# The same instructions in another order: ScalarE and VectorE take turns on the PSUM tile of q and the exponentials

## The chip, the core and the metric

The kernel runs on one core of a Trainium2 chip, in one launch. The metric is the device time of that launch in microseconds; less is better. A core has five engines, each with an instruction line of its own that it works through strictly in order: TensorE (PE in the profile, its weight loads are PEld), VectorE (DVE), ScalarE (ACT), GpSimd (POOL), and SyncE (SP), which here issues all transfers between the chip's memory (HBM) and SBUF. An instruction that needs the result of another engine waits at the head of its engine's line, and everything behind it waits too.

## The reference

One transformer block for 2048 tokens of width 512, in fp32: layer norm, sliding dilated attention (32 heads of 16, eight keys at distance 0, 2, ..., 14), residual, layer norm, a GEGLU feed-forward of width 1792, residual.

```python
qkv = layernorm(x) @ wqkv                      # split into q, k, v, 32 heads of 16
idx = pos[:, None] - 2 * arange(8)[None, :]    # eight keys for each position
logits = einsum("bhsd,bhswd->bhsw", q, k[idx]) * 16 ** -0.5    # masked where idx < 0
o = einsum("bhsw,bhswd->bhsd", softmax(logits), v[idx])
h = x + o @ wo
out = h + (gelu(layernorm(h) @ w_gate) * (layernorm(h) @ w_up)) @ w_down
```

## The kernel before

The tokens are split into four blocks of 512 (numbered 0 to 3). Even and odd positions are kept apart, so that the dilated window is eight rows next to each other. A block passes through projection of q, k and v (L675 to L825), attention (L829), output projection with residual and second layer norm (tail, L931), and the feed-forward. Blocks 0 and 1 run the feed-forward in 14 steps each (ffn_step, L1014), beside the attention of the block after next to them; blocks 2 and 3 run it together with fewer products (early_step L1403, joint L1131, last_sums L1320). Matrix products are made of three matmuls each, of a high and a low part of both operands; the casts to the high part are ScalarE's (L409), the subtraction that gives the low part is VectorE's or GpSimd's (L410).

TensorE has no part in the attention itself. For each of four groups of eight heads, ScalarE copies two rows of q into the tile qp in PSUM (L854), VectorE multiplies them with eight keys (L861, names pk) and adds up over the head's 16 places (L864, into lg). VectorE or GpSimd mask lg (L875), VectorE takes the largest (L877), VectorE or GpSimd subtract it (L878); ScalarE reads one element of it to bring in the exponential's table early (a dummy activation, L881) and writes the exponentials into qp (L883); VectorE sums them (L884), inverts the sum (L886), scales (L887), multiplies with eight values (L903, names pv), and adds these up in three steps by itself or on GpSimd (L908, L910). Tile qp has two halves of 256 values to a partition, taken by groups of heads in turn; both lie in one PSUM tile.

```python
qp = T("qp", [P, 2, 2 * QF], name="qp", pool=psum)
...
i = b % 2
...
act(310, lambda q=q, jj=jj: nc.scalar.copy(
    qp()[:, i].rearrange("p (j f) -> p j f", j=2), q()[:, jj:jj + 2, :]), qrs, [(qp, i)])
```

In a feed-forward step TensorE makes pg and pu from the weights gu (L498), ScalarE takes the gelu of pg into g (L1047), VectorE multiplies g with pu (L1053), ScalarE and GpSimd or VectorE split g into gh and gl (L409, L410), and TensorE adds the product with the down weights to acc (L996 to L998), two steps later. The two banks for pg and pu are taken in turn, so the next step's matmuls need the last step's L1047 and L1053. Weights come from HBM as fraw; ScalarE casts them (L409, L1011, L1025). The low parts of the weights are computed once, written to HBM and read back (ld).

The order is written out. Every operation is recorded by Plan.add (L265) in the program's order with its number; PLACES (L62) holds one number for each of the 2853 operations, and Plan.schedule (L303) sorts the operations by it and emits them in that order, which sets each engine's line. SWAPS lists operations that run on the other of their two possible engines (Plan.swap, L297). Semaphores are set by the layer below, from which instruction touches which tile, in the order of emission.

Of the kernel before, what the change touches and what calls it, by code (L numbers as in the profile page):

```python
# [62 lines left out]
    4765, 17791, 0, 825, 1032, 1239, 1446, 1653, 1860, 2067, 2274, 2481, 2688, 2895, 3102, 3309, 3516, 3723, 3930, 4137, 4344, 4551, 4758, 4965, 5172,  # L63
    5379, 5586, 5793, 6530, 7479, 7589, 7699, 8263, 11601, 28478, 14543, 11401, 26924, 29078, 38112, 40916, 470, 1410, 7001, 8296, 1880, 7857, 8901, 0,
    940, 6146, 6911, 2350, 8712, 10151, 3290, 2820, 3760, 11278, 11938, 4700, 13196, 15673, 5170, 13844, 16923, 4230, 15440, 18748, 20748, 5291, 5291,
    5921, 6611, 6171, 7031, 7526, 10732, 7255, 8382, 11688, 7251, 8206, 4435, 4435, 5000, 5621, 5721, 6041, 6911, 10392, 6306, 7866, 8901, 12118, 12852,
    11072, 12028, 12496, 14292, 14950, 17528, 9568, 10302, 10512, 11348, 12006, 15588, 13188, 13543, 15443, 8036, 8744, 8971, 9652, 10106, 10333, 10560,
    12022, 12930, 13384, 14066, 14968, 15966, 7809, 8517, 9198, 9425, 9879, 10787, 11014, 11796, 12250, 12476, 17238, 19280, 19816, 15648, 15876, 16102,
    16330, 16556, 16784, 17010, 17464, 19734, 19960, 20414, 21548, 21986, 12704, 13158, 13612, 13838, 14740, 15194, 15422, 17692, 18826, 19052, 19506,
    20188, 20624, 22710, 28513, 26633, 27573, 7990, 28618, 29808, 7520, 19291, 19951, 7050, 17266, 28064, 8460, 25014, 25674, 17918, 20642, 24496, 27438,  # L70
    21776, 23590, 25404, 28028, 27218, 28124, 32202, 34270, 22682, 26310, 29482, 32587, 5640, 18133, 19968, 6580, 19353, 25416, 8930, 22341, 25326, 6110,
    20178, 25236, 27124, 27478, 29032, 29692, 13188, 21201, 14448, 22956, 25538, 26924, 22576, 24096, 26488, 28668, 33320, 34404, 31296, 35830, 38552,
    39918, 30388, 33110, 34016, 40508, 36738, 40366, 41272, 42390, 34924, 37644, 39458, 42980, 43704, 45584, 45114, 44174, 9400, 32914, 37358, 40934,
    19808, 31664, 36202, 36862, 40134, 40594, 43174, 45480, 41820, 48894, 46294, 46954, 19338, 38312, 43570, 44230, 23180, 30414, 38762, 41540, 42484,
    43514, 48204, 50144, 44330, 50834, 51638, 52298, 18868, 23526, 24292, 20278, 30182, 30948, 27103, 31956, 35480, 23650, 36726, 37882, 39562, 39916,
    43552, 45486, 42180, 46820, 44908, 58034, 49466, 51048, 52652, 54024, 55606, 60394, 56768, 58350, 64536, 66170, 48094, 50152, 59512, 61094, 55396,
    56978, 62256, 58140, 59722, 63960, 60884, 62466, 65908, 67490, 63662, 64602, 64132, 63192, 74982, 68740, 68270, 69210, 46280, 47188, 50838, 68933,
    44002, 51746, 63628, 68033, 72744, 73652, 74558, 75884, 70024, 70930, 71838, 75294, 77078, 78018, 76608, 77548, 48330, 53548, 60312, 61644, 50270,
    55488, 63756, 64960, 66170, 67550, 68364, 70304, 69523, 70994, 76474, 78806, 53674, 65564, 74768, 75676, 52210, 62894, 72048, 72954, 74330, 76620,
    77300, 78116, 77080, 84356, 78930, 80056, 28043, 39286, 41098, 31804, 44854, 49430, 36336, 52164, 52930, 44644, 53786, 58940, 59798, 64144, 68652,  # L80
    79456, 67280, 87685, 81838, 83858, 75466, 85488, 87070, 91190, 88232, 89814, 94628, 96358, 78652, 80746, 90976, 92558, 83210, 84792, 89604, 86860,
    88915, 91850, 92348, 93930, 96000, 97582, 96066, 94656, 95126, 95596, 99302, 98362, 101102, 98832, 76838, 80930, 93720, 99497, 77744, 80024, 84582,
    100207, 101488, 102394, 103302, 105614, 104208, 105116, 106022, 107140, 108804, 108334, 109274, 107864, 63056, 81336, 82415, 92507, 94520, 95754,
    64282, 72572, 73652, 82590, 90714, 91970, 93910, 95414, 98810, 100906, 96210, 96870, 101366, 108586, 80046, 85382, 90850, 101892, 103512, 111182,
    86326, 87970, 89050, 104036, 106324, 107336, 110162, 110842, 111906, 112366, 111906, 113056, 113636, 114452, 98744, 107730, 97372, 118546, 111464,
    113046, 100116, 114208, 115790, 119206, 116952, 118534, 124309, 131641, 112836, 114418, 119745, 121327, 115580, 117648, 122713, 118373, 119955,
    124541, 121341, 125333, 129309, 130891, 126998, 127938, 126058, 127468, 132891, 132421, 139225, 139695, 106930, 107836, 110558, 134840, 108744,
    109650, 133402, 137290, 141106, 142013, 142920, 151884, 138844, 139751, 144275, 146025, 233320, 159029, 189713, 188773, 26163, 46054, 29144, 30414,
    32738, 35170, 35614, 37940, 34522, 50740, 34860, 43514, 45840, 47410, 48034, 50580, 42144, 42604, 46170, 65390, 47720, 50240, 52774, 53164, 53624,
    56738, 60394, 66860, 55830, 59254, 69054, 76960, 77606, 78958, 91240, 97679, 99500, 52680, 58154, 60838, 61754, 68490, 68623, 70684, 73010, 54798,  # L90
    58694, 64620, 95046, 65080, 68150, 75204, 76280, 79506, 81996, 85606, 87546, 77300, 88236, 90720, 93220, 96734, 99772, 108320, 112431, 116196, 65072,
    83745, 82280, 82725, 85490, 87660, 88360, 93218, 81306, 84930, 86856, 100087, 90404, 90850, 97018, 98242, 98702, 101246, 105436, 106646, 101806,
    104296, 106042, 110502, 110962, 112041, 116380, 119124, 121282, 98120, 101246, 103606, 106204, 105304, 106646, 107106, 107496, 107956, 115056, 116802,
    118546, 112246, 117406, 119866, 120592, 121117, 121551, 121996, 124085, 125023, 125468, 109744, 122923, 123583, 90380, 123448, 126083, 117862, 123973,
    124833, 117392, 124498, 126688, 121327, 126588, 127495, 128402, 129519, 130244, 131551, 131761, 132116, 133310, 133895, 134975, 138279, 143386,
    144046, 125681, 130681, 131588, 132705, 133775, 134510, 134720, 135075, 135760, 136345, 137425, 140794, 142551, 143291, 132495, 134309, 135216,
    136830, 137555, 138290, 138500, 138855, 139681, 136123, 137030, 137937, 139054, 140146, 140881, 141091, 141446, 142196, 140658, 142061, 142686,
    143827, 144485, 145110, 122656, 78488, 150450, 131499, 145715, 148040, 148040, 150235, 153045, 116922, 96536, 118332, 120545, 122336, 127293, 143076,
    155240, 158610, 156494, 158050, 158730, 178238, 160215, 162883, 163343, 163733, 164193, 166738, 173548, 174923, 166738, 169098, 170358, 172858,
    175738, 176818, 191227, 194519, 204608, 148730, 156309, 169063, 170123, 171183, 173658, 179758, 181328, 184138, 161410, 162323, 166398, 192999,  # L100
    166858, 170238, 173388, 175853, 176313, 180613, 187243, 191573, 178518, 190433, 197953, 201233, 205193, 206273, 210523, 212840, 215053, 143521,
    170003, 180843, 182498, 187848, 192133, 190392, 194328, 197138, 189743, 191573, 193513, 206138, 195044, 199938, 201233, 202668, 206548, 212023,
    213768, 214713, 203128, 205858, 209468, 214373, 215173, 216253, 219775, 223076, 225823, 199938, 201503, 202668, 208498, 203483, 205333, 206278,
    208753, 209213, 215658, 217403, 218128, 218008, 221318, 227373, 228583, 218943, 219600, 222392, 223601, 227033, 229043, 229700, 234030, 236573,
    237018, 154180, 158695, 153690, 139779, 126528, 130974, 138380, 140269, 140971, 131809, 136225, 143991, 140165, 145182, 146089, 146996, 147903,
    148810, 149717, 148350, 152440, 153165, 155244, 138755, 144975, 145635, 146615, 148135, 145500, 146885, 149510, 148260, 150624, 151531, 152438,
    153345, 154252, 155159, 154670, 157445, 158170, 160805, 141696, 150834, 151494, 151359, 152744, 150255, 153994, 155839, 164415, 156066, 156973,
# [1436 lines left out]
```

## Time and profile before

| what | before |
|---|---|
| median of three runs | 626.97 us (624.17 to 627.29) |
| the profiled execution's own time | 625.67 us |
| its span, first to last instruction | 623.9 us |
| weight loads of TensorE | 499.9 us busy |
| mean rate of the transfers | 248 GB/s, 154.51 MB |
| granted TensorE clock | 1.00 |

The span is what the trace covers; the 1.8 us beside it lie around the first and the last instruction. Busy time of an engine counts its instructions' own time. A matmul's end is modelled and overlaps the next one's start, so that the distance from start to start tells TensorE's pace. In the views of the prediction a row names the engine, the line of the kernel, the tile written and, behind an arrow, the tiles read, without buffer numbers; the idle time of an engine before an instruction stands with the instruction or transfer that ended it.

### The profile page before, as it was taken

The page shows a single profiled execution, that of the slowest core. Times are in us where ns is not written, and L with a number is a line of the kernel's source. Part 1 is how long each engine was busy: PE and PEld are TensorE (multiplying, and loading weights), DVE is VectorE, ACT ScalarE, POOL GpSimd, SP SyncE. Part 2 cuts the span into 40 slices and gives each one's busy share as a digit, 9 for nine tenths or more (in the row PEclk, how much of TensorE's full clock was granted, in tenths as well). Part 3 has the DMA queues.
Part 4 walks back from the last instruction along what each step waited for, and adds up shares of the span by engine and source line. Part 5 has one row for each costly group of instructions (what it writes and reads, how often), then busy time and mean ns, then how long its engine had stood idle before and what let it go on. Part 6 is the DMA issues. An engine that isn't in the chain of part 4 may idle for free.

```text
span 623.9 us, 8388 instructions
## 1 busy us (share of the span) xinstructions
PE 610.5 (98%) x2696; PEld 499.9 (80%) x2696; DVE 534.4 (86%) x674; ACT 440.5 (71%) x765; POOL 349.4 (56%) x327
## 2 busy tenths in 40 slices
PE   8999999999999899999999999999999999999997
PEld 7888788887877778887888878888777888888885
DVE  6889999989989898999999899747978887778862
ACT  5787598748456766796886869789865675568841
POOL 5589897525888845766484683304124433443562
PEclk9999999999999999999999999999999999999999
DMA  8758588689998898979999889967489655758984
GB/s 297 229 178 299 191 241 231 179 274 301 342 267 297 255 291 278 285 234 336 334 318 342 245 235 275 311 181 217 129 235 260 225 195 176 221 163 238 245 237 119
DMA packets 106365, 154.51 MB, mean 248 GB/s; under 512 B 47296, under 2 KB 60352, under 8 KB 105936
## 3 DMA queue, kind: packets, MB, share of 16 engines
q1 hardware_dynamic: 106320, 153.97, 79.6%
q8 instruction: 21, 0.34, 0.2%
q14 instruction: 24, 0.20, 0.1%
HBM read 107.48 MB, written 36.23 MB: 230 GB/s over the span
## 4 chain that ended last, share of the span: by engine, by line
PE 65%; DMA 12%; DVE 6%; ACT 6%; POOL 5%; issue 4%; SPq 1%; DVEq 0%; ACTq 0%; POOLq 0%
PE dn L1316 10%; PE pa L1198 8%; DMA fraw<-in_wffn_dram 8%; PE qkv L498 7%; PE pu L498 6%; PE pg L498 5%; PE wo L498 5%; PE pc L1198 5%; PE qka L757 4%; PE acc L996 2%; PE acc L997 2%; PE acc L998 2%; PE qkc L757 2%; PE qkv L491 2%; DMA gu<-ld 1%
## 5 line engine op out<-in xcount | busy, mean ns | idle before, releaser
L861 DVE TENSOR_TENSOR pk<-kw,qp 128x2048 f32<-128x2048 f32 x32 | 72.9, 2280 | 4.5 <-ACT qp L854 3.1
L903 DVE TENSOR_TENSOR pv<-vw,qp 128x2048 f32<-128x2048 f32 x32 | 72.6, 2281 | 3.0 <-ACT qp L883 1.4
L864 DVE TENSOR_REDUCE lg<-pk 128x128 f32<-128x2048 f32 x32 | 72.7, 2274 | 0.2
L908 POOL TENSOR_TENSOR pv<-pv 128x512 f32<-128x512 f32 (+1 forms) x36 | 65.6, 1831 | 11.0 <-DVE pv L903 7.4
L498 PE MATMUL pu<-hTh,gu 128*128 128x512 f32 x224 | 60.3, 391 | 2.8 <-DVE g L1053 2.8
L498 PE MATMUL pg<-hTh,gu 128*128 128x512 f32 x224 | 60.2, 390 | 0.8 <-DMA gu<-ld 0.5
L498 PEld LDWEIGHTS pu<-hTh,gu 128*128 128x128 f32 x224 | 41.8, 188 | 12.7 <-DVE g L1053 4.1
L498 PEld LDWEIGHTS pg<-hTh,gu 128*128 128x128 f32 x224 | 41.8, 188 | 10.4 <-DMA gu<-ld 0.9
L996 PE MATMUL acc<-dnh,gh 128*128 128x512 f32 x112 | 43.6, 389 | 0.0
L997 PE MATMUL acc<-dnl,gh 128*128 128x512 f32 x112 | 43.6, 389 | 0.0
L998 PE MATMUL acc<-dnh,gl 128*128 128x512 f32 x112 | 43.6, 389 | 0.0
L410 POOL TENSOR_TENSOR gu<-fraw,gu 128x512 fp32r<-128x512 f32 x21 | 27.1, 1298 | 20.4 <-ACT gu L409 14.3
L410 POOL TENSOR_TENSOR gl<-g,gh 128x512 fp32r<-128x512 f32 x23 | 30.0, 1304 | 14.5 <-ACT gh L409 14.4
L910 POOL TENSOR_TENSOR o<-pv 128x256 f32<-128x256 f32 x25 | 21.3, 856 | 26.7 <-DVE pv L908 14.8
L1198 PE MATMUL pa<-tt,jh 128*128 128x512 f32 x112 | 30.3, 393 | 0.9 <-ACT gr_xhat L1223 0.7
L498 PE MATMUL pu<-hTl,gu 128*128 128x512 f32 x112 | 30.0, 389 | 0.0
L498 PE MATMUL pg<-hTl,gu 128*128 128x512 f32 x112 | 29.9, 389 | 0.0
L908 DVE TENSOR_TENSOR pv<-pv 128x1024 f32<-128x1024 f32 (+1 forms) x28 | 29.6, 1072 | 0.1
L1228 ACT COPY jt<-pa 128x512 f32<-128x512 f32 x32 | 18.7, 585 | 12.3 <-PE pa L1198 10.3
L409 ACT CAST gu<-fraw 128x512 fp32r<-128x512 f32 x28 | 16.8, 617 | 14.0 <-DMA fraw<-in_wffn_dram 13.0
L477 POOL TENSOR_SCALAR rs_h<-mv_h 128x1 f32<-128x1 f32 x16 | 4.6, 291 | 39.0 <-DVE mv_h L476 38.9
L1198 PEld LDWEIGHTS pa<-tt,jh 128*128 128x128 f32 x112 | 20.8, 188 | 6.3 <-ACT gr_xhat L1223 1.1
(496 smaller groups left out, 1834.0 us busy)
## 6 DMA issues: line engine op xcount, KB each, us to landing
fraw<-in_wffn_dram SPq DMA_DIRECT2D x47, 768.0 KB, 6.0
kw<-kv SPq DMA_DIRECT2D x16, 704.0 KB, 6.0
vw<-kv SPq DMA_DIRECT2D x16, 704.0 KB, 6.4
gu<-ld SPq DMA_DIRECT2D x19, 512.0 KB, 5.6
kv<-qkvt SPq DMA_DIRECT2D x32, 256.0 KB, 3.1
ld<-gu SPq DMA_DIRECT2D x14, 512.0 KB, 5.2
ws<-sums_kw SPq DMA_DIRECT2D x21, 256.0 KB, 2.2
x<-in_x_dram SPq DMA_DIRECT2D x16, 256.0 KB, 5.4
```

The lines of the kernel that those rows point to most:

```text
L410: sub = lambda eng: eng.tensor_tensor(lo(), src(), hi().bitcast(F32), op=ALU.subtract)
L498: nc.tensor.matmul(acc(), a, b, start=(p == k == 0 and not seeded), stop=(p == n - 1 and k == KD - 1), skip_group_check=seeded)
L757: nc.tensor.matmul(acc(), a(k), b()[:, k], start=first and q == k == 0, stop=q == 2 and k == 1, skip_group_check=not first)
L861: nc.vector.tensor_tensor(pr(), k4, q2.unsqueeze(2).to_broadcast([P, 2, W, QF]), op=ALU.mult)
L864: dve(2195, lambda pr=pr, jj=jj: nc.vector.tensor_reduce(lg()[:, i, jj:jj + 2], pr().rearrange("p j w (h d) -> p j w h d", d=DH), axis=AX. ...
L903: nc.vector.tensor_tensor(pr().rearrange("p j w (h d) -> p j w h d", d=DH), v5, e5, op=ALU.mult)
L908: either(home, 256 * m, lambda eng, pr=pr, m=m: eng.tensor_tensor(pr()[:, :, 0:m], pr()[:, :, 0:m], pr()[:, :, m:2 * m], op=ALU.add), [], ...
L996: nc.tensor.matmul(a, gh()[:, sl], dh(), start=(i == 0 and not SEED), stop=False, skip_group_check=SEED)
L997: nc.tensor.matmul(a, gh()[:, sl], dl(), start=False, stop=False, skip_group_check=SEED)
L998: nc.tensor.matmul(a, gl()[:, sl], dh(), start=False, stop=(i == NF - 1), skip_group_check=SEED)
L1198: nc.tensor.matmul(acc(), a[:, k], b(k), start=first and p == k == 0, stop=p == 2 and k == 1, skip_group_check=not first)
L1316: nc.tensor.matmul(acc(), a[0]()[:, cols], b[0](), start=first and q == 0, stop=last and q == 2, skip_group_check=True)
```

## The change

Only the two tables are different. 2245 of the 2853 numbers of PLACES have other values, and 210 operations change between two engines that can both run them (102 from VectorE to GpSimd, 96 back, 12 between ScalarE and VectorE). The operations, their operands, tiles and buffers are the same. By the tables' own numbers, a write of ScalarE to qp and a use of qp by VectorE overlap in 18 cases before, always with different halves, and in none in the change.

```diff
 PLACES = (
-    4765, 17791, 0, 825, 1032, 1239, 1446, 1653, ...
+    0, 16788, 0, 825, 1032, 1239, 1446, 1653, ...
 ...
 SWAPS = (
-    47, 50, 51, 54, 62, 65, 79, 89, 169, 172, 175, ...
+    47, 50, 51, 54, 59, 62, 65, 68, 76, 92, 172, ...
```

The orders below are those of the built programs, one row for each instruction: line, operation, tile written and tiles read with their numbers, shape. In the names, pk_1_2_0 is the product of block 1, heads' group 2, rows 0 and 1; g_0_3 is the g of block 0, step 3. The attention of block 1 and the feed-forward of block 0 run side by side.

**First place: the exponentials of group 1 of block 1.** VectorE before, from the first product with the values of group 0 on:

```order
L903 TENSOR_TENSOR pv_1_0_0_1736<-vw_1_0_1603,qp_421 128x2048
L878 TENSOR_TENSOR lg_456<-lg_456,ms_559 128x256
L903 TENSOR_TENSOR pv_1_0_2_1757<-vw_1_0_1603,qp_421 128x2048
L908 TENSOR_TENSOR pv_1_0_2_1757<-pv_1_0_2_1757 128x2x512
L884 TENSOR_REDUCE ms_559<-qp_421 128x32
L1053 TENSOR_TENSOR g_0_3_1765<-pu_0_3_1760,g_0_3_1765 128x512
L861 TENSOR_TENSOR pk_1_2_0_1799<-kw_1_2_1666,qp_421 128x2048
L886 RECIPROCAL ms_559<-ms_559 128x32
L864 TENSOR_REDUCE lg_456<-pk_1_2_0_1799 128x128
L887 TENSOR_TENSOR qp_421<-qp_421,ms_559 128x256
```

and in the change, from the second of these products on:

```order
L903 TENSOR_TENSOR pv_1_0_2_1752<-vw_1_0_1315,qp_406 128x2048
L410 TENSOR_TENSOR gl_0_2_1767<-g_0_2_1705,gh_0_2_1754 128x512
L877 TENSOR_REDUCE ms_553<-lg_440 128x32
L410 TENSOR_TENSOR dnl_0_4_1775<-fraw_0_4_1656,dnh_0_4_1744 128x512
L410 TENSOR_TENSOR gu_0_4_1724<-fraw_0_4_1656,gu_0_4_1724 128x512
L878 TENSOR_TENSOR lg_440<-lg_440,ms_553 128x256
L908 TENSOR_TENSOR pv_1_0_2_1752<-pv_1_0_2_1752 128x2x512
L861 TENSOR_TENSOR pk_1_2_0_1803<-kw_1_2_1619,qp_406 128x2048
L1053 TENSOR_TENSOR g_0_3_1765<-pu_0_3_1760,g_0_3_1765 128x512
L864 TENSOR_REDUCE lg_440<-pk_1_2_0_1803 128x128
L884 TENSOR_REDUCE ms_553<-qp_406 128x32
L861 TENSOR_TENSOR pk_1_2_2_1851<-kw_1_2_1619,qp_406 128x2048
```

The sum over the exponentials (L884) stood right behind the additions of pv_1_0_2 and ahead of g_0_3; now the product pk_1_2_0 and g_0_3 stand ahead of it. ScalarE in the same place, before:

```order
L883 ACTIVATE qp_421<-lg_456 128x256
L409 CAST gu_0_4_1715<-fraw_0_4_1653 128x512 x2
L883 ACTIVATE qp_421<-lg_456 128x256
L1047 ACT_TABLE_LOAD
L1047 ACTIVATE g_0_3_1765<-pg_0_3_1738 128x512
L409 CAST dnh_0_4_1777<-fraw_0_4_1653 128x512
L409 CAST gh_0_2_1782<-g_0_2_1701 128x512
L854 COPY qp_421<-q_1_2_1586 128x256
L409 CAST gu_0_5_1811<-fraw_0_5_1745 128x512
L433 COPY a_o_1_0_0_1836<-o_1_0_1813 128x1024
```

and in the change:

```order
L1047 ACTIVATE g_0_3_1765<-pg_0_3_1737 128x512
L854 COPY qp_406<-q_1_2_1675 128x256
L409 CAST gu_0_5_1786<-fraw_0_5_1731 128x512 x2
L881 ACT_TABLE_LOAD
L881 ACTIVATE warm_68<-ms_553 128x1
L409 CAST dnh_0_5_1816<-fraw_0_5_1731 128x512
L883 ACTIVATE qp_406<-lg_440 128x256
L854 COPY qp_406<-q_1_2_1675 128x256
L1047 ACT_TABLE_LOAD
L1047 ACTIVATE g_0_4_1841<-pg_0_4_1811 128x512
```

The exponentials in question are the second row of L883 before (the first is that of group 0) and the only one in the change. They stood ahead of the gelu of g_0_3 and of the first copy of q_1_2; now they stand behind both, and behind a load of the table with its dummy activation.

**Second place: the exponentials of group 3 of block 1.** VectorE before:

```order
L887 TENSOR_TENSOR qp_421<-qp_421,ms_559 128x256
L903 TENSOR_TENSOR pv_1_2_2_2090<-vw_1_2_1775,qp_421 128x2048
L884 TENSOR_REDUCE ms_559<-qp_421 128x32
L1053 TENSOR_TENSOR g_0_7_2060<-pu_0_7_2055,g_0_7_2060 128x512
L886 RECIPROCAL ms_559<-ms_559 128x32
L903 TENSOR_TENSOR pv_1_2_0_2122<-vw_1_2_1775,qp_421 128x2048
L887 TENSOR_TENSOR qp_421<-qp_421,ms_559 128x256
L903 TENSOR_TENSOR pv_1_3_0_2153<-vw_1_3_1884,qp_421 128x2048
```

and in the change:

```order
L887 TENSOR_TENSOR qp_406<-qp_406,ms_553 128x256
L877 TENSOR_REDUCE ms_553<-lg_440 128x32
L903 TENSOR_TENSOR pv_1_2_2_2078<-vw_1_2_1797,qp_406 128x2048
L410 TENSOR_TENSOR gu_0_8_2008<-fraw_0_8_1965,gu_0_8_2008 128x512
L1053 TENSOR_TENSOR g_0_7_2060<-pu_0_7_2054,g_0_7_2060 128x512
L884 TENSOR_REDUCE ms_553<-qp_406 128x32
L903 TENSOR_TENSOR pv_1_2_0_2121<-vw_1_2_1797,qp_406 128x2048
L886 RECIPROCAL ms_553<-ms_553 128x32
```

g_0_7 has moved from behind the sum (L884) to ahead of it.

**Third place: the first product of block 2.** VectorE before:

```order
L908 TENSOR_TENSOR pv_1_3_0_2153<-pv_1_3_0_2153 128x2x256
L903 TENSOR_TENSOR pv_1_3_2_2228<-vw_1_3_1884,qp_421 128x2048
L861 TENSOR_TENSOR pk_2_0_0_2250<-kw_2_0_2143,qp_421 128x2048
L1053 TENSOR_TENSOR g_0_9_2220<-pu_0_9_2207,g_0_9_2220 128x512
L864 TENSOR_REDUCE lg_456<-pk_2_0_0_2250 128x128
L410 TENSOR_TENSOR gl_0_8_2300<-g_0_8_2145,gh_0_8_2176 128x512
```

and in the change:

```order
L908 TENSOR_TENSOR pv_1_3_0_2155<-pv_1_3_0_2155 128x2x256
L410 TENSOR_TENSOR oTl_1_2141<-a_o_1_1_0_2076,oTh_1_2132 128x512
L903 TENSOR_TENSOR pv_1_3_2_2227<-vw_1_3_2029,qp_406 128x2048
L410 TENSOR_TENSOR gu_0_10_2218<-fraw_0_10_2123,gu_0_10_2218 128x512
L1053 TENSOR_TENSOR g_0_9_2215<-pu_0_9_2202,g_0_9_2215 128x512
L410 TENSOR_TENSOR gu_0_10_2218<-fraw_0_10_2123,gu_0_10_2218 128x512
L908 TENSOR_TENSOR pv_1_3_2_2227<-pv_1_3_2_2227 128x2x512
L861 TENSOR_TENSOR pk_2_0_0_2274<-kw_2_0_1882,qp_406 128x2048
L410 TENSOR_TENSOR dnl_0_10_2295<-fraw_0_10_2123,dnh_0_10_2239 128x512
L864 TENSOR_REDUCE lg_440<-pk_2_0_0_2274 128x128
```

The product pk_2_0_0, which reads qp, stood ahead of g_0_9; now it stands behind it, with a subtraction and an addition between.

The line of SyncE is also in another order throughout, with the same transfers. The line of ScalarE holds 30 loads of an activation table, before 28.

328 rows, old and new, of tables (PLACES, SWAPS) are left out of this document.

## The prediction

> **What bounds the kernel now.** First the page: the span, and each engine's busy time.
>
> ```profile
> span 623.9 us, 8388 instructions
> PE 610.5 (98%) x2696; PEld 499.9 (80%) x2696; DVE 534.4 (86%) x674; ACT 440.5 (71%) x765; POOL 349.4 (56%) x327
> ```
>
> TensorE is not busy for 623.9 - 610.5 = 13.4 us and has the same 2696 matmuls to do in any order, so a change of order is worth at most what it does to those 13.4 us. Next the view of waits for TensorE alone: who waited for whom, total us, times, longest.
>
> ```profile
> PE pu L498 <- DVE g L1053: 2.8, 3, 1.6
> PE warm_ps L396 <- POOL ident masks.py:199: 1.3, 1, 1.3
> PE pg L1420 <- ACT m_sh L1425: 0.9, 1, 0.9
> PE wo L498 <- ACT wo L951: 0.8, 1, 0.8
> PE qkc L757 <- DVE qkvt L772: 0.7, 1, 0.7
> PE pa L1198 <- ACT gr_xhat L1223: 0.7, 1, 0.7
> PE tp_x L559 <- DVE xhat_x L550: 0.7, 2, 0.5
> PE pg L498 <- DMA gu<-ld: 0.5, 1, 0.5
> PE pa L1198 <- ACT jt L1228: 0.4, 1, 0.4
> PE pg L498 <- ACT gu L409: 0.3, 1, 0.3
> ```
>
> These sum to 9.1 us; the other 4.3 lie after the last matmul and in gaps too short for this view. The largest entry is the feed-forward step's product g (L1053) on VectorE, late three times. The timeline shows why (start, us, engine and line; in brackets the idle time before and who ended it). The first place:
>
> ```profile
> 168.88 2.28 DVE L903 TENSOR_TENSOR pv<-vw,qp 128x2048 f32<-128x2048 f32 x1
> 171.20 0.39 ACT L883 ACTIVATE qp<-lg 128x256 f32<-128x256 f32 x1 [5.39 <-DVE pv L903]
> 174.43 0.38 ACT L854 COPY qp<-q 128x256 f32<-128x256 f32 x1
> 174.84 0.42 DVE L884 TENSOR_REDUCE ms<-qp 128x32 f32<-128x256 f32 x1 [2.41 <-ACT qp L854]
> 175.18 0.68 DVE L1053 TENSOR_TENSOR g<-pu,g 128x512 f32<-128x512 f32 x1
> ...
> 185.29 0.68 DVE L1053 TENSOR_TENSOR g<-pu,g 128x512 f32<-128x512 f32 x1
> 185.46 0.38 ACT L854 COPY qp<-q 128x256 f32<-128x256 f32 x1 [2.73 <-DVE pv L903]
> 186.03 1.21 PE L498 MATMUL pu<-hTh,gu 128*128 128x512 f32 x4 [0.51 <-DVE g L1053]
> 188.20 0.38 ACT L854 COPY qp<-q 128x256 f32<-128x256 f32 x1 [1.05 <-DVE pk L861]
> 192.12 1.21 PE L498 MATMUL pg<-hTh,gu 128*128 128x512 f32 x4 [0.32 <-ACT gu L409]
> ```
>
> The exponentials (L883) of one half of tile qp start 0.04 us after VectorE's multiply with the other half ends (168.88 + 2.28 = 171.16), after an idle 5.39 us: the two halves are not used by both engines at once. Then VectorE's sum (L884) over the finished exponentials waits 2.41 us for a copy (L854) into the other half. VectorE is now 2.4 us behind, ScalarE likewise, and both pass it on: g is late at 186.03, ScalarE's cast gu at 192.12. The second and third places are plainer:
>
> ```profile
> 210.34 1.28 ACT L883 ACT_TABLE_LOAD   x1 [3.45 <-DVE pv L903]
> 210.43 1.07 PE L498 MATMUL pg<-hTh,gu 128*128 128x512 f32 x4
> 211.64 0.39 ACT L883 ACTIVATE qp<-lg 128x256 f32<-128x256 f32 x1
> 212.06 0.42 DVE L884 TENSOR_REDUCE ms<-qp 128x32 f32<-128x256 f32 x1 [1.79 <-ACT qp L883]
> 212.40 0.68 DVE L1053 TENSOR_TENSOR g<-pu,g 128x512 f32<-128x512 f32 x1
> 213.13 1.20 PE L498 MATMUL pu<-hTh,gu 128*128 128x512 f32 x4 [1.64 <-DVE g L1053]
> ...
> 227.06 0.38 ACT L854 COPY qp<-q 128x256 f32<-128x256 f32 x1 [0.71 <-DVE pv L903]
> 227.47 2.29 DVE L861 TENSOR_TENSOR pk<-kw,qp 128x2048 f32<-128x2048 f32 x1 [0.44 <-ACT qp L854]
> 229.67 0.68 DVE L1053 TENSOR_TENSOR g<-pu,g 128x512 f32<-128x512 f32 x1
> 230.41 0.96 PE L498 MATMUL pu<-hTh,gu 128*128 128x512 f32 x3 [0.65 <-DVE g L1053]
> ```
>
> Each time g stands on VectorE right behind an instruction that waits for qp, and TensorE waits for g.
>
> **The change part by part.** *qp in turns.* What a wait of TensorE costs: a group of four lasts 1.07 us undisturbed (210.43) and 1.20 behind a wait (213.13), so 0.13 more; and a matmul shows 0.39 us (1.07 less three steps of 0.227) while the next is due after 0.227, so the time counted as idle begins 0.16 us after the loss does. Cost = idle + 0.29. The four waits that hang on qp are the three for g (2.8) and the one for gu L409 (0.3): 3.1 + 4 x 0.29 = **4.3 us**. In the changed order the cause is gone at all of them: at the first place the exponentials come after the copy for the next product, and the sum L884 stands behind g_0_3 and not ahead of it; at the second g_0_7 stands ahead of the sum, and the table load sits in front of a dummy activation (L881) that reads no PSUM; at the third g_0_9 stands ahead of the product L861 that waits for the copy. So g no longer waits for qp there, and what is late next is a transfer, since the same stretch loads the weights. Bounds: 0, if other instructions get stuck on qp instead, and 4.3 plus the waits for qkvt L772 and wo L951 (0.7 + 0.8 + 2 x 0.29 = 2.1), whose engines also run late in the attention stretch, together 6.4. I take 4.3, which is the part whose chain the rows show.
>
> *Added waits.* At the first place L883 now follows VectorE's product of q; if it reaches ScalarE's front early, a copy L854, a table load and the gelu of g_0_4 are queued behind it, and g_0_4 for TensorE behind them. One product is 2.28 us long (168.88); the step of g_0_4 comes 10 us after that of g_0_3 in the rows above (175.18, 185.29), so I cost it at nothing; without that cover it is up to 2.3 us.
>
> *Engine swaps.* The orders hold 4 instructions fewer on VectorE, 6 more on GpSimd, 2 fewer on ScalarE. GpSimd is idle for 44% of the span, and the two engines on which TensorE waits lose work: nothing, with 1 us either way as an estimate (two waits of the 0.3 to 0.5 us kind in the list).
>
> *Table loads.* The orders hold 28 loads before and 30 after. One takes 1.28 us, and the activation follows 1.30 us after its start (210.34 to 211.64): 2 x 1.3 = 2.6 us more on an engine that is idle for 29% of the span. Covered: 0; uncovered 2.6. The Trainium skill (ScalarE: Activation LUTs, What ACT_TABLE_LOAD costs) puts a switch at about 2.66 us, a load and a drain of 1.38 us; by that the two would be an estimated 5.3 us. The rows show no such drain behind the load, so the sum keeps 0.
>
> *Transfers.* The queue's order changes everywhere. The windows of the attention stretch (TensorE, weight load, VectorE, ScalarE, GpSimd busy; clock, DMA share, GB/s) and one wait of ScalarE say how much room there is:
>
> ```profile
> 140.00:400.00 260.00, 255.56 (x1124) 209.14 (x1123) 243.82 (x232) 191.81 (x303) 168.19 (x146) 1.00 0.93 289
> 300.00:350.00 50.00, 50.00 (x222) 41.40 (x221) 48.02 (x38) 37.81 (x62) 32.29 (x26) 1.00 0.99 317
> ...
> ACT dnh L1011 <- DMA fraw<-in_wffn_dram: 3.3, 1, 3.3
> ```
>
> Taking 4.3 us out of 260 brings the share of 0.93 to about 0.945; at 300 to 350 there is no room at all. TensorE has one wait for a transfer now (gu<-ld, 0.5 + 0.29 = 0.8). I add **one more such wait, 0.8 us**; bounds 0 and three weight loads of 3.3 us late (9.9).
>
> *The start, the joint stage of the last two blocks, the end.* All of it is ordered anew, at equal work. The waits there now are tp_x, m_sh, gr_xhat, jt: 2.7 us, with 0.29 each for five 4.2 us. They could go or double; I take no change, with 3 us either way.
>
> **The sum.** 625.67 (the profiled execution, 1.8 more than its span) - 4.3 + 0.8 = **622.2 us**. The median of the three runs, 626.97, lies 1.3 us above the profiled execution; against it the forecast is 0.8% faster. A difference under 0.5% can hardly be told from none here, so the bounds are 623.8 and 630.1.
>
> **The rivals.** *The waits only move.* ScalarE still writes qp 48 times and VectorE uses it 96 times, and the two halves still exclude each other. VectorE's waits on qp now (the view of waits of VectorE alone):
>
> ```profile
> DVE pk L861 <- ACT qp L854: 3.1, 6, 0.7
> ...
> DVE ms L884 <- ACT qp L883: 2.7, 3, 1.8
> ...
> DVE ms L884 <- ACT qp L854: 2.4, 1, 2.4
> ...
> DVE pv L903 <- ACT qp L883: 1.4, 2, 0.7
> ```
>
> That is 9.6 us in twelve waits, and TensorE felt them at four places. If as many fall ahead of a g in the new order, the time stays at 625.7. For it: VectorE is 94% busy in the window above (243.82 of 260), so any wait soon reaches g. Against it: the three places shown have lost their cause. Chance 0.22.
>
> *The transfers become the bound: slower.* The place is the stretch 280 to 350, where the DMA engines are at 0.99 and ScalarE once waited 3.3 us for fraw. A TensorE that comes 4.3 us sooner asks for the same bytes sooner. It decides once more than two weight loads land later than ScalarE's slack: three at 3.3 us give 621.4 + 9.9 = 631.3, slower than before. Against it: the share over the whole stretch stays under 1. Chance 0.12.
>
> *ScalarE pays for the table loads.* If both extra loads fall ahead of a gelu that TensorE needs soon, 621.4 + 2.6 = 624.0. Against it: ScalarE waits far longer than that in the same stretch (5.39, 3.45, 2.73 above). By the page of the Trainium skill named above it would be an estimated 626.7. Chance 0.06.
>
> **How the numbers follow.** The forecast, 622.2, has 0.60 and its own range of 618.5 to 625.5 (the 3 us of the redrawn stages, a little more above for the transfers). The other cases give 624.0 (0.06), 625.7 (0.22) and 631.3 (0.12). Range for 8 in 10: 617.5 to 629.5; below lies the upper bound of the qp term, above most of the transfers' case. Faster by over 0.5% (under 623.8): 0.48 of the forecast's 0.60, 0.05 of the unmoved case, 0.03 of the table loads, 0.56. Slower (over 630.1): the transfers' case and a little of the rest, 0.12. Within 0.5%: 0.32.
>
> **What would show it.** In the profile after: TensorE's waits for g L1053 nearly gone (under 1 us) and for gu L409 too; the exponentials L883 with idle of under 1 us behind a multiply L903; VectorE's waits on qp under 4 us. The transfers' step is right if TensorE's waits for gu<-ld or casts of fraw sum to about 1.3 us. The prediction is wrong if g L1053 still leads TensorE's waits, if a cast of fraw does, or if the joint stage (430 to 480 us) loses over 6 us where it now loses about 3.

## The result, and the profile after

| | before | changed | ratio, 95% interval |
|---|---|---|---|
| median, us | 625.80 (8 runs) | 622.19 (8 runs) | 0.9943 [0.9920, 0.9965] |
| lowest to highest, us | 624.17 to 628.90 | 621.10 to 623.50 | |
| profiled execution, us (span) | 625.67 (623.9) | 623.48 (621.7) | |

The changed kernel is 0.6% faster. The page of the changed kernel, busy times:

```profile
span 621.7 us, 8392 instructions
PE 611.5 (98%) x2696; PEld 501.7 (81%) x2696; DVE 534.8 (86%) x670; ACT 443.4 (71%) x765; POOL 356.8 (57%) x333
```

TensorE is not busy for 621.7 - 611.5 = 10.2 us where it was 13.4. The view of waits for TensorE in the changed kernel, complete:

```profile
PE pa L1198 <- ACT gr_r L1223: 3.0, 1, 3.0
PE warm_ps L396 <- POOL ident masks.py:199: 1.3, 1, 1.3
PE pg L498 <- ACT g L1047: 0.6, 1, 0.6
PE qka L757 <- ACT qkvt L767: 0.5, 1, 0.5
PE wo L498 <- ACT wo L951: 0.3, 1, 0.3
PE pa L1198 <- ACT gr_xhat L1223: 0.2, 1, 0.2
```

They sum to 5.9 us, before 9.1. The three waits for g L1053 and the one for gu L409 are gone. Three are new: 0.5 us for qkvt L767, where before had 0.7 for qkvt L772; 0.6 us for the gelu of g (L1047), which will matter below; and 3.0 us for gr_r in the joint stage. The same view for VectorE and for ScalarE, the entries on qp:

```profile
DVE ms L884 <- ACT qp L883: 3.4, 4, 1.1
DVE pk L861 <- ACT qp L854: 1.5, 3, 0.9
```

```profile
ACT qp L854 <- DVE pv L903: 9.5, 4, 4.7
ACT qp L883 <- POOL lg L878: 2.2, 2, 1.3
ACT qp L854 <- DVE pk L861: 2.2, 3, 0.9
```

VectorE waits 4.9 us for qp in place of 9.6. ScalarE's copies wait longer for VectorE's multiply L903 than before (9.5 us; 4.0 before), but its exponentials no longer wait for that multiply (5.4 us before). So the turns are still taken, and what stands behind them has changed. The second of the three places, in the changed kernel (timeline: start, us, engine, line, in brackets the idle time before and its end):

```profile
206.87 1.14 ACT L409 CAST gu<-fraw 128x512 fp32r<-128x512 f32 x2
...
208.03 1.28 ACT L881 ACT_TABLE_LOAD   x1
208.15 0.68 DVE L1053 TENSOR_TENSOR g<-pu,g 128x512 f32<-128x512 f32 x1
209.32 0.20 ACT L881 ACTIVATE warm<-ms 128x1 f32<-128x1 f32 x1
209.43 0.37 ACT L883 ACTIVATE qp<-lg 128x256 f32<-128x256 f32 x1
...
209.83 0.43 DVE L884 TENSOR_REDUCE ms<-qp 128x32 f32<-128x256 f32 x1 [1.00 <-ACT qp L883]
```

VectorE still waits 1.00 us for the exponentials, but g is done at 208.83, ahead of that wait. Where TensorE gained is seen in the windows (TensorE, weight load, VectorE, ScalarE, GpSimd busy; clock, DMA share, GB/s), first of before, then of the changed kernel:

```profile
140.00:240.00 100.00, 96.88 (x426) 78.41 (x425) 91.72 (x90) 66.56 (x109) 70.62 (x58) 1.00 0.90 287
240.00:430.00 190.00, 188.68 (x832) 155.34 (x832) 166.55 (x171) 150.16 (x238) 103.53 (x98) 1.00 0.90 280
430.00:480.00 50.00, 47.81 (x206) 37.58 (x205) 41.76 (x92) 36.69 (x77) 14.90 (x18) 1.00 0.75 210
```

```profile
140.00:240.00 100.00, 99.33 (x439) 81.18 (x439) 94.08 (x89) 70.36 (x113) 75.70 (x63) 1.00 0.92 289
240.00:430.00 190.00, 189.70 (x837) 156.08 (x837) 168.32 (x178) 152.09 (x242) 112.89 (x102) 1.00 0.92 278
430.00:480.00 50.00, 46.85 (x200) 37.67 (x199) 39.46 (x86) 33.03 (x69) 14.55 (x18) 0.97 0.77 200
```

From 140 to 240 us TensorE is busy 2.45 us longer, from 240 to 430 another 1.0; in the joint stage it loses 1.0 and there the granted clock is 0.97. The number in brackets counts the matmuls: 439 in the first stretch, where before has 426.

### The profile page after: what moved, and what is told of

Its sections match the earlier page's. It is cut to its first block, busy times and chain, and to the rows that moved or that the text cites. A ratio compares the mean times of both kernels' runs of the same rounds, so it can differ in the third digit from the quotient of the medians.

```text
span 621.7 us, 8392 instructions
## 1 busy us (share of the span) xinstructions
PE 611.5 (98%) x2696; PEld 501.7 (81%) x2696; DVE 534.8 (86%) x670; ACT 443.4 (71%) x765; POOL 356.8 (57%) x333
## 4 chain that ended last, share of the span: by engine, by line
PE 68%; DMA 9%; POOL 7%; DVE 6%; ACT 5%; issue 4%; SPq 0%; DVEq 0%; ACTq 0%; POOLq 0%
PE dn L1316 10%; PE pa L1198 8%; PE pu L498 7%; PE pg L498 7%; PE qka L757 5%; DMA fraw<-in_wffn_dram 4%; PE qkv L498 4%; PE wo L498 4%; PE pc L1198 4%; PE acc L997 3%; PE acc L998 3%; PE acc L996 3%; PE pg L1420 2%; PE pu L1420 2%; PE qkv L491 2%
## 5 line engine op out<-in xcount | busy, mean ns | idle before, releaser
L908 POOL TENSOR_TENSOR pv<-pv 128x1024 f32<-128x1024 f32 (+1 forms) x42 | 79.9, 1908 | 25.4 <-DVE pv L908 12.6
L903 DVE TENSOR_TENSOR pv<-vw,qp 128x2048 f32<-128x2048 f32 x32 | 72.2, 2282 | 1.5 <-DMA vw<-kv 0.8
L498 PEld LDWEIGHTS pg<-hTh,gu 128*128 128x128 f32 x224 | 41.7, 188 | 10.2 <-ACT g L1047 1.0
L410 POOL TENSOR_TENSOR gl<-g,gh 128x512 fp32r<-128x512 f32 x22 | 29.7, 1352 | 9.6 <-ACT gh L409 9.6
L410 POOL TENSOR_TENSOR gu<-fraw,gu 128x512 fp32r<-128x512 f32 x21 | 27.5, 1319 | 10.1 <-ACT gu L409 10.1
L409 ACT CAST gu<-fraw 128x512 fp32r<-128x512 f32 x28 | 16.5, 618 | 18.7 <-DMA fraw<-in_wffn_dram 9.2
L908 DVE TENSOR_TENSOR pv<-pv 128x512 f32<-128x512 f32 (+1 forms) x22 | 23.6, 1074 | 1.3 <-POOL pv L908 1.2
L498 PEld LDWEIGHTS pg<-hTl,gu 128*128 128x128 f32 x112 | 21.0, 188 | 4.4
L498 PEld LDWEIGHTS pu<-hTl,gu 128*128 128x128 f32 x112 | 21.0, 188 | 4.4
```

The source lines that it names most:

```text
L410: sub = lambda eng: eng.tensor_tensor(lo(), src(), hi().bitcast(F32), op=ALU.subtract)
L498: nc.tensor.matmul(acc(), a, b, start=(p == k == 0 and not seeded), stop=(p == n - 1 and k == KD - 1), skip_group_check=seeded)
L903: nc.vector.tensor_tensor(pr().rearrange("p j w (h d) -> p j w h d", d=DH), v5, e5, op=ALU.mult)
L908: either(home, 256 * m, lambda eng, pr=pr, m=m: eng.tensor_tensor(pr()[:, :, 0:m], pr()[:, :, 0:m], pr()[:, :, m:2 * m], op=ALU.add), [], ...
```

## The experiments

Five timed rounds each; runs of one group shared a chip and their runs of before. In the experiments' kernels, e5 apart, the tables fill fewer lines, so that their line numbers are some 36 to 43 lower (L1053 is L1010 in the first). The measure used throughout is TensorE's busy time from 140 to 240 us, the stretch of the three places: 96.88 in before, 99.33 in the changed kernel.

### Three products moved (e1)

On VectorE, in the order of before (line numbers of before):

```diff
-L884 TENSOR_REDUCE ms<-qp 128x32
 L1053 TENSOR_TENSOR g_3<-pu_3,g_3 128x512
+L884 TENSOR_REDUCE ms<-qp 128x32
...
-L884 TENSOR_REDUCE ms<-qp 128x32
 L1053 TENSOR_TENSOR g_7<-pu_7,g_7 128x512
+L884 TENSOR_REDUCE ms<-qp 128x32
...
-L861 TENSOR_TENSOR pk_0_0<-kw_0,qp 128x2048
 L1053 TENSOR_TENSOR g_9<-pu_9,g_9 128x512
+L861 TENSOR_TENSOR pk_0_0<-kw_0,qp 128x2048
```

> The tables of before with three places moved and nothing else: three instructions of ScalarE that make g tiles (g_0_3, g_0_7, g_0_9) stand just ahead of the exponentials, row sum or product that shares the q tile and waited there. Theory (the waiting q instructions hold back g, TensorE waits for g): the three TensorE waits for g of L1053 (2.8 us in before) fall under 1 us, and the time falls by 2 to 3.7 us, to 622.1 to 623.8 against a before of 625.8. Rival (the wait only moves to the next g, or to VectorE): the sum of TensorE waits stays near 9 us and the time within 1 us of before.

(The three are VectorE's products L1053, as the rows show; the expectation names the wrong engine.) Measured: 623.33 us, ratio 0.9969 [0.9954, 0.9984]. TensorE's waits in this kernel:

```profile
PE tp_h L378 <- DVE xhat_h L436: 0.9, 1, 0.9
...
PE pu L455 <- DVE g L1010: 0.6, 1, 0.6
...
PE acc L955 <- DVE gl L367: 0.5, 1, 0.5
...
PE pg L455 <- ACT g L1004: 0.3, 1, 0.3
PE pg L455 <- ACT gu L366: 0.3, 1, 0.3
```

The waits for g fell from 2.8 to 0.6 us as the theory had it. The 0.6 us is the wait of the first place, at 186.13 us, which is as long as before (0.51), and the wait for gu behind it stays too: to put g_0_3 ahead of the sum was not enough there. The gelu (217 us) and gl (224 us) are late instead; tp_h is late at 142 us, ahead of the moved products, and so not by them. The median is 1.9 us lower by the ratio, just under what the theory gave. This profile doesn't show where it comes from: the stretch has 97.18 us busy, only 0.3 more than before, and the first 140 us, whose order is that of before, have 1.4 more (138.65 and 137.26). A part of the wait did move on: the engines are still stopped by qp, and something else stands behind them.

### The change in one half of the program only (e2, e3)

The tables joined at 240 us: e2 has the changed order ahead of it, e3 behind it.

> The changed order for all that stands before 240 us in the tables, the order of before from there on. Theory (the gain is made where g waits were, up to 240 us): 3.5 us of the gain is there, 621.5 to 623 against 625.8, and the q waits of VectorE in 170 to 240 us shrink as in the changed kernel. Rival (the redrawing of 240 to 440 us makes the gain): within 1 us of before.

> The order of before up to 240 us, the changed order from there on. Theory: the early waits stay (TensorE waits for g near 2.8 us), 240 to 440 us gives 2 us and the joint stage takes 1 to 3 us of it back: 624.5 to 627 against 625.8. Rival (the gain is made after 240 us): 622 to 623.

Measured: e2 629.64 us, 1.0076 [1.0051, 1.0101]; e3 625.81 us, 1.0002 [0.9986, 1.0018]. In e3 the new order from 240 us on gains nothing by itself; that the joint hides a gain there is not ruled out. e2 does not bring the rest as its expectation had it. Ahead of the joint it shows a gain: in the stretch TensorE is busy 97.90 us (96.88 in before), though it waits 2.1 us for a gelu of g. But the joint opens a stall of its own, right behind it:

```profile
249.42 2.00 ACT L391 COPY a_h<-xhat_h 128x1024 uint16<-128x1024 uint16 x2 [4.93 <-DVE xhat_h L437]
251.32 1.14 ACT L367 CAST gu<-fraw 128x512 fp32r<-128x512 f32 x2
253.62 1.34 ACT L397 COPY a_h<-xhat_h 128x1024 uint16<-128x1024 uint16 x1 [1.17 <-DMA xhat_h<-a_h]
...
256.38 0.58 ACT L909 COPY wo<-h 128x512 f32<-128x512 f32 x1
```

The copy that seeds wo stands in ScalarE's line behind 4.93 + 1.17 us of waiting, and TensorE waits 4.04 us for it at 257 us. The joint is a place that neither plan foresaw, so e2 can't be read as the first half's worth. Its windows show something else, which returns below: after that idle TensorE's granted clock is 0.66 for 10 us.

```profile
255.00:265.00 10.00, 7.99 (x22) 6.38 (x23) 5.77 (x6) 6.51 (x11) 6.25 (x6) 0.66 0.97 285
265.00:270.00 5.00, 5.00 (x23) 4.13 (x22) 4.58 (x6) 3.42 (x5) 2.68 (x4) 1.00 0.30 62
```

### The sharing removed, the order kept (e4, e8)

Two ways to end the turns without moving an instruction. e4 puts one half of qp into SBUF:

```diff
+    qp1 = T("qp1", [P, 2 * QF], name="qp1", pool=tiny)
+    half_of = lambda i: qp1() if i else qp()[:, 0]
...
-                    qp()[:, i].rearrange("p (j f) -> p j f", j=2), q()[:, jj:jj + 2, :]), qrs, [(qp, i)])
+                    half_of(i).rearrange("p (j f) -> p j f", j=2), q()[:, jj:jj + 2, :]), qrs, [own(i)])
```

> The order of before, with the second half of the q tile in an SBUF tile of its own (1 KB a partition), so that the two engines need take no turns on it. Theory (turns on one PSUM tile are the cause): VectorE's q waits fall from 9.6 to under 4 us, TensorE's waits for g go, and the time falls by 3 to 4.5 us to 621 to 623. Rival 1 (the waits are true dependences, not the sharing): within 1 us of 625.8. Rival 2 (SBUF operands cost VectorE more than PSUM ones, by its port shared with GpSimd): L861 and L903 take over 2.45 us each on the odd blocks, and the time is over 626.5.

Measured: 662.18 us, 1.0588 [1.0562, 1.0614], the second rival. Two groups of e4:

```profile
L820 DVE TENSOR_TENSOR pk<-kw,qp 128x2048 f32<-128x2048 f32 x32 | 82.8, 2588 | 9.7 <-ACT qp L813 5.8 <-POOL o L869 2.7 <-DMA kw<-kv 0.9
...
L367 POOL TENSOR_TENSOR gl<-g,gh 128x512 fp32r<-128x512 f32 x23 | 39.5, 1721 | 5.6 <-ACT gh L366 5.6
```

In every second group of heads the multiply now has both operands in SBUF. Over all groups it takes 2588 ns in the mean (2280 before), its slowest 4505, and GpSimd's subtraction 1721 (1304 before). The slowest multiply and what GpSimd does beside it:

```profile
97.97 5.70 POOL L867 TENSOR_TENSOR pv<-pv 128x1024 f32<-128x1024 f32 x2
98.04 4.50 DVE L820 TENSOR_TENSOR pk<-kw,qp 128x2048 f32<-128x2048 f32 x1 [2.71 <-POOL o L869]
```

The multiply starts 0.07 us after an addition of GpSimd does and lasts 2.2 us longer than before, about the length of that addition (2452 ns in the mean before): the two engines hold each other up. The Trainium skill (SBUF — State Buffer, SBUF: two separate sides) says that a VectorE instruction with two SBUF inputs and a GpSimd instruction lock the same ports, one waiting for the whole of the other; the trace agrees. So q is in PSUM for a reason, and this run says nothing on the turns.

e8 takes a PSUM bank instead, the one of wo, which lies empty from 137 to 225 us and again from 254 to 319 in the plan:

```diff
+        ax = T("aux", [P, 2 * QF], name=f"qx_{c}", pool=psum) if c in (1, 2) else None
...
+            far = ax is not None and b % 2 == 1
+            eh, own = (lambda: ax() if far else qp()[:, i]), ((ax, None) if far else (qp, i))
...
-            act(310, lambda: nc.scalar.activation(e4(), lv(), AF.Exp, scale=SCALE), whole, [(qp, i)], table="exp")
+            act(310, lambda: nc.scalar.activation(e4(), lv(), AF.Exp, scale=SCALE), whole, [own], table="exp")
```

> The order of before, with the exponentials of the odd groups of blocks 1 and 2, and the q of their last group, in a PSUM bank that is empty then. Theory (sharing of one PSUM tile makes the waits): the TensorE waits for g near 186 and 213 us (1.3 and 1.6 us) go, VectorE's q waits lose half of their 9.6 us, and the time falls by 1.5 to 3 us against before, to 622.5 to 624. Rival (true dependences, or the next wait takes over): within 1 us of before.

Measured: 620.05 us against 624.74, 0.9924 [0.9903, 0.9944]. (The row of the prediction has 0.51 us at 186 us, not the expectation's 1.3.) It is 4.7 us faster with the order of before, more than expected. The first place again, in e8:

```profile
169.18 2.27 DVE L867 TENSOR_TENSOR pv<-vw,qp 128x2048 f32<-128x2048 f32 x1
169.29 0.39 ACT L845 ACTIVATE qx<-lg 128x256 f32<-128x256 f32 x1 [2.94 <-DVE lg L840]
...
172.63 0.42 DVE L846 TENSOR_REDUCE ms<-qx 128x32 f32<-128x256 f32 x1
172.97 0.68 DVE L1017 TENSOR_TENSOR g<-pu,g 128x512 f32<-128x512 f32 x1
```

The exponentials of one half (now tile qx) run beside the multiply with the other half (qp), wait only for their own logits, and the sum L846 has no wait. The stretch in e8:

```profile
140.00:240.00 100.00, 99.62 (x444) 81.94 (x443) 95.43 (x94) 70.05 (x116) 73.96 (x62) 1.00 0.96 304
```

TensorE is busy 99.62 of 100 us, and no wait for g is left in its list. It starts 444 matmuls, 18 more than in before; at 0.227 us each these are 4.1 us. VectorE still waits 5.4 us for the tiles of q (9.6 before), 4.2 of them for copies of q. This is the run that shows the cause: two engines that use one PSUM tile, not the order as such. It gives the odd half a tile and a bank of its own at once, so it doesn't tell whether the tile or the bank makes them take turns.

### The joint stage (e5, e6, e7)

e5 is the changed kernel once more. e6 moves one instruction of it on ScalarE; e7 has the changed order up to 430 us and the old one behind it.

```diff
+L1223 ACTIVATE gr_r<-pa_0 128x512
 L1178 CAST jh<-sums_kw 128x512
 L1178 CAST jh<-fraw_3 128x256
 L409 CAST sums_kw<-sums_kw 128x256
-L1223 ACTIVATE gr_r<-pa_0 128x512
```

> The changed kernel once more, unaltered, as a second profile beside the others. Theory (the joint stage's stall is part of the order): TensorE again stands about 3 us near 460 us for gr_r of L1223 and runs some 8 matmuls at 0.43 us behind it, time 622. Rival (that stall is one execution's chance): the stall is under 1 us, time still near 622.

> The changed kernel with one instruction moved: the gelu that makes gr_r (L1223) for the matmul that stalls at 460 us goes ahead of the jh cast of ScalarE that waits for a transfer there. Theory: the stall falls from 3.05 to about 1.5 us, the slow matmuls behind it go as well, and the time falls by 1.5 to 3.5 us against the changed kernel, to 618.7 to 620.7. Rival (the matmul behind it waits for the same transfer, or the stall is rare): within 1 us of the changed kernel.

> The changed order up to 430 us, the order of before in the joint stage and after. Theory (the change is 4.4 us ahead at 430 us and gives 1.7 us back in the joint stage): 620 to 621.5. Rival (the old joint stage finds its tiles and transfers at other moments and stalls, as the seam at 240 us did): over 624, with a new TensorE wait of over 2 us between 430 and 480 us.

Measured, all against 624.74: e5 622.44, 0.9984 [0.9961, 1.0007]; e6 623.00, 0.9970 [0.9948, 0.9992]; e7 621.73, 0.9956 [0.9936, 0.9976]. In e5's profile the wait for gr_r is 1.0 us and not 3.0, and the joint stage has 48.02 of 50 us busy (47.81 in before): the 3 us stall was that execution's, and the rival of e5 holds. The interval of e5 holds 1: in this set of runs the changed kernel by itself can't be told from before, while e6 and e7, which have its order up to the joint stage, are clear of 1. e6 and e7 can't be told from e5. The joint stage is neither where the change gains nor where it loses steadily.

The median of e5 agrees with the first (622.19), but three of its twelve executions took 625.8 to 628.4 us, with a granted clock of 0.995 to 0.997 over the whole span. The profile of e6, whose order is that of the changed kernel up to the joint stage, caught such an execution (624.83 us, clock 0.996). Its ScalarE, then its TensorE:

```profile
188.23 0.62 ACT L366 CAST dnh<-fraw 128x512 fp32r<-128x512 f32 x1
193.11 0.62 ACT L366 CAST gu<-fraw 128x512 fp32r<-128x512 f32 x1 [4.26 <-DMA ld<-gu]
193.63 0.59 ACT L1004 ACTIVATE g<-pg 128x512 f32<-128x512 f32 x1
...
194.27 1.20 PE L455 MATMUL pg<-hTh,gu 128*128 128x512 f32 x4 [3.51 <-ACT g L1004]
195.31 1.81 PE L455 MATMUL pg<-hTl,gu 128*128 128x512 f32 x4
196.91 1.91 PE L455 MATMUL pg<-hTh,gu 128*128 128x512 f32 x4
```

A cast into a gu tile waits for the store of what that tile held (ld<-gu), and the gelu that TensorE needs stands behind it. TensorE idles 3.51 us and then needs 1.81 and 1.91 us for groups that take 1.07. In the changed kernel's own profile the same wait is the 0.6 us for g L1047, in e5 0.9, in e7 1.0, in e2 2.1. In before this gelu stands ahead of the cast (190.96 us, the cast at 196.77): the wait is one that the change brought.

### That gelu put back ahead of the cast (e9 to e12)

e9 moves one instruction of ScalarE in the changed kernel:

```diff
 L409 CAST dnh_6<-fraw_6 128x512
-L409 CAST gu_7<-fraw_7 128x512
 L1047 ACTIVATE g_5<-pg_5 128x512
+L409 CAST gu_7<-fraw_7 128x512
 L409 CAST gu_7<-fraw_7 128x512
```

> The changed kernel with one instruction moved: g_0_5 of L1047 goes ahead of ScalarE's cast that makes a gu tile of filter group 7 (L409), which waits near 190 us for a transfer. Theory (the change moved that cast ahead of g, so that a late transfer now stops TensorE there, for 0.6 to 3.5 us and now and then with slow matmuls behind it): the TensorE wait for g near 191 us goes, the time falls by about 1 us to a ratio near 0.994, and the slowest executions stay under 625. Rival (the next tile waits for the same transfer): the stall is found again within 5 us, the time as the changed kernel's, ratio 0.996 to 0.998.

> The same, with the exponentials of the odd groups of blocks 1 and 2, and the q of their last group, in the PSUM bank that is empty then. Theory (in the changed order the shared tile no longer stops TensorE): within 1 us of the run before it. Rival (turns still cost something there): 1.5 to 3 us less, as from before to the free bank.

> The order of before up to 430 us with the free bank, and the changed order from there on. Theory (the free bank takes the q waits, and the changed joint stage costs TensorE about 1 us less than the old one): 618.5 to 620, ratio 0.990 to 0.992. Rival (the joint stage is the same either way or worse): 620 to 622.

> The places of before, with the changed kernel's choice of engine for the 210 operations that may run on either. Theory (which engine runs them costs nothing by itself): within 1 us of before, ratio 0.998 to 1.002. Rival (an operation on another engine in the old order makes that engine late): slower by over 2 us, with TensorE waits for tiles of L409 and L410 that before has not.

Measured, all against 625.05: e9 620.41 us, 0.9935 [0.9912, 0.9958]; e10 621.94, 0.9944 [0.9927, 0.9962]; e11 621.43, 0.9947 [0.9929, 0.9965]; e12 658.36, 1.0536 [1.0515, 1.0558].

In e9 the place reads so:

```profile
188.22 0.59 ACT L1004 ACTIVATE g<-pg 128x512 f32<-128x512 f32 x1
...
190.68 1.07 PE L455 MATMUL pg<-hTh,gu 128*128 128x512 f32 x4
191.15 1.15 ACT L366 CAST gu<-fraw 128x512 fp32r<-128x512 f32 x2 [2.33 <-DMA ld<-gu]
```

The cast still waits 2.33 us, but TensorE runs on, and its stretch is full (100.00 of 100 us). What that is worth in time the runs don't settle: e9's ratio can't be told from the changed kernel's first (0.9943) and lies below that of e5 (0.9984). Of the 44 executions with the cast ahead (the changed kernel's 8, e5, e6, e7) 13 had a clock under 0.998; of the 23 of e9 and e10 one had, of 74 of before one. At least one of the 13 lost its clock elsewhere: the changed kernel's profiled one (0.997), at 460 us. e9's slowest execution, 625.65, is that one, so the bound of 625 was just missed. e10 shows no further gain from the free bank with the new order; its median is 1.5 us above that of e9, outside the 1 us of its theory, but the intervals overlap. e11 was meant to add two gains and did not: against e8 the changed joint stage brings nothing. e12 shows that the choice of engine belongs to the order: with the old places it costs 33 us, and TensorE waits for tiles of L410 (gl 3.5 us, and others) that it did not wait for before, as its rival said. The best of all are e8 and e9, 620.05 and 620.41 us, which the intervals can't tell apart.

## Why the prediction was right, point by point

The forecast was 622.2 us and the median is 622.19. That the two agree so closely is luck: the interval of the ratio allows 2.2 to 5.0 us of gain, the median of e5 lies 2.3 us below its own before, and in the sum a wait that was not foreseen takes the place of one that was.

- **qp in turns, 4.3 us.** Right in mechanism and about right in size. e8 keeps the order, takes away the turns that held up g, and gains 4.7 us, 4.1 us of matmuls in the stretch. The four waits named are gone in the changed kernel; its 13 more matmuls are 3.0 us, and the new wait for the gelu (0.6 + 0.29) takes most of the rest. e1 bears it out less well: its median falls by 1.9 us, but its profile doesn't show that gain in the stretch. How the change does it was half as foreseen: the exponentials no longer wait for a multiply, but VectorE's waits for qp are 4.9 us, not under 4, and ScalarE's copies wait more (9.5 us). The order puts these waits where no g stands behind them.
- **Added waits, nothing; transfers, 0.8 us.** The step on added waits failed as it was put. It named the exponentials behind the product of q, which cost nothing, and overlooked the gelu put behind a cast that waits for a store. The transfer term had the right kind and about the right size in three of the five profiles with that order (0.6, 0.9 and 1.0 us of idle; 2.1 and 3.5 in the others), by another way: TensorE's waits for gu<-ld are gone, and the transfer reaches it through ScalarE and g. In the worst profile the idle alone was 3.51 us, with slow matmuls behind it.
- **A wait costs idle + 0.29 us.** No run contradicts it for idles of up to 2.10 us, behind which no matmuls are slow. Behind one of 2.75 us and more it is too low by 1.4 us and more, as below.
- **Engine swaps, nothing.** Not separable: e12 shows that away from their places they cost 33 us, so their share can't be taken alone.
- **Table loads, nothing.** No run took them alone. In before ScalarE idled 8.6 and 5.2 us just ahead of the loads of L883 and L1047; after, 1.5 and 0.2, and 0.1 ahead of those of L881 (eight, before five), and TensorE waits for none of them. The 1.3 us of the sum is the whole price here: at the second place the load starts at 208.03 us, 0.02 us after the cast ahead of it ends (206.87 + 1.14), and its activation follows at 209.32, so that no drain of 1.38 us shows on either side.
- **Start, joint stage, end, no change.** Right within the 3 us. In the first 140 us TensorE is busy 138.16 us in the changed kernel and 138.65 in e1, which has the order of before there; for the joint stage and the end e3, e5 and e7 show no steady gain or loss.
- **The rivals.** The waits only move: true of a small part (e1, and the gelu at 191 us). Transfers as the bound at 280 to 350 us: not seen; TensorE is busy 189.70 of 190 us from 240 to 430. Table loads that make ScalarE late: not seen either, as above.

What stays open is whether the shared tile or the shared bank makes the engines take turns, where e1's gain lies, why the store ld<-gu lands late in some executions and not in others, and how many of the executions with a low clock stalled at 191 us; only profiled ones can be seen.

## What to carry to other kernels

When two engines wait for each other and their data do not, look for a PSUM tile that both use, and try a bank that is empty at that time before you reorder anything: here a few lines did at least as much as a whole new order (ratios 0.9924 and 0.9943, whose intervals overlap). When an order is redrawn, list for each instruction that the busiest engine needs soon what now stands ahead of it on its engine and may wait for a transfer. A wait like that shows as 0.6 us in one profile and 3.5 in another, so look at the spread of the executions and their clock, not at one profile.

## What the hardware showed that was not expected

A TensorE that idles long enough loses its clock. The windows of the changed kernel's profile around the stall at 460 us:

```profile
452.00:460.00 8.00, 4.95 (x23) 3.76 (x21) 4.84 (x11) 3.74 (x10) 0.48 (x1) 1.00 1.13 164
460.00:464.00 4.00, 4.00 (x11) 3.14 (x12) 2.06 (x4) 2.29 (x4) 2.60 (x4) 0.58 0.74 258
464.00:468.00 4.00, 4.00 (x19) 3.31 (x18) 3.35 (x7) 2.89 (x7) 0.42 (x1) 1.00 0.64 165
```

Eleven matmuls in 4 us after the idle of 3.05 us, 19 in the next 4. Over all profiles, eight idles of 2.75 us and more (2.75 in e12, 3.03 in e4, up to 4.04 in e2) were each followed by some 7 to 14 matmuls 0.427 us apart in place of 0.227, which is an estimated 1.4 to 2.8 us more (7 and 14 times 0.2); none of 2.10 us and less was. So a long stall costs more than its length. The Trainium skill (TensorE: Matmul & The Clock Gate, Part 1: The HAM clock gate) puts the loss of the clock at an idle window of about 3.4 us; the halved pace agrees, and here 2.75 us were enough.
